# A fused sliding-window attention and gated projection: q and k turned by VectorE, scores in four 32-row parts of TensorE, v loaded in overlapping blocks

## The chip, the cores and the metric

The kernel runs on one core of one Trainium2 chip. The metric is the device time of one launch in microseconds (us), taken over several executions; the profile describes one execution and gives its span from the first to the last instruction. The engines are named as in the profile: PE (TensorE matmuls), PEld (its weight loads), DVE (VectorE), ACT (ScalarE), POOL (GpSimd) and SP (SyncE, which only issues DMAs here).

## The reference

There are 8 batches, 8 heads, 576 positions and a head size of 64. Heads 0 to 3 ("plain") see the last 32 positions; heads 4 to 7 ("dilated") see 32 positions at steps of 4. The attention output of the eight heads, side by side, is x (8 x 576 x 512), which goes into a gated unit: a causal depthwise convolution of 5 taps gives the gate, a 512 x 512 matmul gives the values, and a second one gives the output.

```python
scores = scale * np.matmul(q, k.transpose(0, 1, 3, 2))
mask_plain = (rel >= 0) & (rel < window)                                   # window 32
mask_dil = (rel >= 0) & (rel < window * dilation) & (rel % dilation == 0)  # dilation 4
attn = softmax(np.where(masks, scores, -1e9))
x = matmul(attn, v) as (B, S, H * D)
gate_pre[:, s] = sum over k of conv_w[k] * x[:, s - 4 + k]
out = (sigmoid(gate_pre) * (x @ w_val)) @ w_out
```

## The kernel before

**Order.** Nothing is looped in program order. Each piece of work is a `Task` with an engine (or a choice of two), an assumed duration, a priority, the buffers (`Ten`) that it takes and the tasks that it needs. `Plan.run` is a list scheduler: it picks one task after the other by the earliest start, then by priority, assigns buffers, and the order so found is the order of each engine's queue. Priorities are the batch number plus offsets in `TUNE` by kind of task. Where the plan sees TensorE idle, it puts up to six idle matmuls on a tile `warm` (L803) ahead of a task. All loads and stores go through SP's one queue; a load waits until the third load before it has landed (`depth` 3).

**Attention of one batch.** Work is in blocks of 96 queries against 128 keys (the 96 and 32 before them), six blocks in a sequence; a dilated head is four interleaved sequences of 144 positions. For the plain heads `load_p` (L433) brings q and k as two strips of 2304 bytes per partition; 18 TensorE transposes per tensor (L548) turn them into one PSUM tile, and two copies by ACT or DVE (L465, L467) put them into `qT` and `kT`, two heads to a tile of 128 rows. For the dilated heads `load_d` (L443, L447) brings rows of 1024 bytes, and five transposes (L613) and one copy serve each half. `attend` runs six score matmuls per half sequence, two heads in two 64-row parts of the array (L486), exp on ACT (L493), the mask on DVE or POOL (L500), 12 matmuls with v (L509, the row sums come from an added column of ones), and the reciprocal and scaling on DVE (L518, L519).

**v.** A block needs its 96 rows and the 32 before it. `load_vp` (L458, pieces of 256 bytes) and `load_vd` (L452, pieces of 1024 bytes) bring the 96 rows to partitions 32 to 127; a copy by POOL or ACT (`halo`, L465 or L469) then fills partitions 0 to 31 from partitions 96 to 127 of the block before. The dilated v is cast to bf16 (`vn`).

**Back to rows of x.** Transposes of `xn` (L573, L639) and copies to `xT` follow, one per pair of heads, four per batch.

**Gated unit.** For each half batch of 288 positions and each pair of 128 channels: 20 convolution matmuls (L669), tanh on ACT (L679), 8 value matmuls (L687), and the product on DVE into `yT` (L697). `outputs` takes 128 rows at a time: 4 matmuls with `w_out` (L715), a copy to `osb` (L723, L725), a store of 256 KB (L729); 36 of them.

**PSUM** is three tiles of two banks (`ps2`) and two of one bank (`ps1`).

Of the kernel before, what the change touches and what calls it, by code (L numbers as in the profile page):

```python
# [15 lines left out]


TUNE = {'seed': 193001,
 'jit': 0,
 'lag': 2.021,  # L20
 'plain': 0.646,
 'unit': -0.629,
 'half': -0.321,
 'chunk': 0.345,
 'look': {'PE': 0, 'ACT': 0.233, 'DVE': 0.13, 'POOL': 0.697, 'SP': 0.591},
 'flex': 0.338,
 'switch': 0.02,
 'conv': -1.304,
 'wv': 1.403,
 'wo': 2.062,  # L30
 'bufs': {'ps2': 3,
          'ps1': 2,
          'qk': 8,
          'vp': 3,
# [4 lines left out]
          'et': 5,  # L39
          'xn': 4,  # L40
          'gate': 3,
          'osb': 5,
          'xT': 4,
          'yT': 3},
 'kind': {'G': -0.357,
          'Xd': -1.057,
          'Ad': 0.509,
          'Sp': -4.69,
          'Tqp': -0.992,
          'Ap': -0.173,  # L50
          'Ekd': -1.272,
          'Eqd': 1.89,
          'ST': -1.836,
          'Y': 0.794,
          'Ed': 1.871,
          'Wv': -0.423,
          'Lqd': 0.297,
          'C': -1.069,
          'Lqp': -0.075,
          'Tqd': -1.649,  # L60
          'Lvp': 0.148,
          'Fp': 4.197,
          'U': 2.107,
          'H': 3.76,
          'Ep': -0.793,
          'Md': 1.981,
          'Ct': 3.963,
          'Xp': -0.118,
          'Tkd': 0.572,
          'Fd': -1.123,  # L70
          'Nd': 0.276,
          'Lc': -0.608,
          'Lwo': 2.324,
          'Sd': -0.312,
          'Wo': 1.347,
          'early': 1.617,
          'EO': -0.437,
          'Cd': 1.31,
          'Ekp': -4.677,
          'Tkp': -2.543,  # L80
          'Np': 1.144,
          'Lvd': 0.762,
          'Eqp': -2.532,
          'Lkr': -0.445,
          'Lkp': 0.146,
          'Mp': -2.525,
          'Lqr': 0.066,
          'Lwv': -0.03,
          'Lkd': -0.161,
          'V': -0.623,  # L90
          'O': 0.244},
 'depth': 3,
 'heat': 6,
 'page0': 440,
 'lookq': 3.0}


def hi_bf16(ap: bass.AP) -> bass.AP:
# [15 lines left out]
class Task:  # L114
    def __init__(self, name, eng, fn, deps=(), tens=(), prio=0.0, mode=None, xfer=0.0, n=1, act=0.0, out=None):
        self.name = name
        self.eng = eng
        self.fn = fn
        self.deps = [d for d in deps if d is not None]
        self.tens = [t for t in tens if t is not None]  # L120
# [8 lines left out]
        self.end = None  # L129
        self.users = []  # L130
        self.missing = len(self.deps)
        for d in self.deps:
            d.users.append(self)
        for t in self.tens:
            t.left += 1


class Plan:
# [3 lines left out]
    WIN, HOT, PAGE, FETCH = 3.4134, 0.40, 256, 1.1  # L142
    HEAT = 0.2133

    def __init__(self, counts):
        self.tasks = []
        self.free = {c: [0.0] * n for c, n in counts.items()}
# [7 lines left out]
        self.heats = 0  # L155
        self.act = {}
        self.slow = {}
        self.count = 0
        self.pages = {}
        self.bound = TUNE["page0"]  # L160
        self.rnd = random.Random(TUNE["seed"])

    def add(self, *a, **k):
        t = Task(*a, **k)
        kind = "".join(takewhile(str.isalpha, t.name))
        t.prio += TUNE["kind"].get(kind, 0.0) + self.rnd.uniform(-1.0, 1.0) * TUNE["jit"]
        self.tasks.append(t)
        return t

    def emit(self, t, eng):  # L170
        t.fn(eng)

    def ready(self, t, eng):
        r = 0.0
        for d in t.deps:
            if d.on == SP or d.on == eng:
                e = d.end
            else:
                e = d.end + self.LAT[d.on]
            if e > r:  # L180
                r = e
# [14 lines left out]
    def pe_run(self, s, dur, act, n):  # L196
        t, i0 = s, self.count
        page = (i0 - self.bound) // self.PAGE + 1
        marks = []
        while self.bound + page * self.PAGE <= i0 + n:  # L200
            marks.append(((self.bound + page * self.PAGE - i0) / n, page))
            page += 1
        marks.append((1.0, None))
        done = 0.0
        for frac, p in marks:
            part = max(0.0, frac - done)
            while part > 1e-9:
                w = int(t / self.WIN)
                f = self.speed(w)
                end = (w + 1) * self.WIN  # L210
                need = part * dur * f
                step = min(need, end - t)
                if step < 1e-9:
                    step, end = min(need, self.WIN), end + self.WIN
                g = step / need * part
                self.act[w] = self.act.get(w, 0.0) + act * g
                t += step
                part -= g
            done = max(done, frac)
            if p is not None:  # L220
                t = max(t, self.pages.get(p, 0.0))
                wait = 1.1 + min(max(0.0, self.dma - t), TUNE["lookq"])
                self.pages[p + 1] = t + wait + self.FETCH
        self.count += n
        return t

    def run(self):
        cand = [t for t in self.tasks if t.missing == 0]
# [3 lines left out]
        depth = TUNE["depth"]  # L232
        look, flex, sw = TUNE["look"], TUNE["flex"], TUNE["switch"]
        while n:
            best = None
            for t in cand:
                if t.load and t is not self.loads[0]:
                    continue
                for eng, dur in t.eng.items():
# [9 lines left out]
                    if eng == PE and t.mode != self.mode:  # L249
                        at += sw  # L250
# [10 lines left out]
            after = None  # L261
            if t.load:
                self.loads.pop(0)
                after = self.landed[-depth] if len(self.landed) >= depth else None
                self.landed.append(t)
            gap0 = self.clock[eng]
            for x in t.tens:
                if x.idx is None:
                    f = self.free[x.cls]
                    x.idx = min(range(len(f)), key=lambda i: f[i])  # L270
                    if x is t.tens[0] or x.cls in ("ps1", "ps2"):
# [3 lines left out]
            t.heat = 0  # L275
            if eng == PE:
                if t.out is not None and t.mode is not None:
                    h, at = 0, gap0
                    while h < TUNE["heat"] and at + self.HEAT * self.speed(int(at / self.WIN)) < s - 0.05:
# [4 lines left out]
                        at = self.pe_run(at, self.HEAT, self.HEAT, 2)  # L284
# [5 lines left out]
                    self.heats += h  # L290
                if t.mode != self.mode:
                    s += 0.09
                self.mode = t.mode
                e = self.pe_run(s, dur, t.act, 2 * t.n + 2)
# [19 lines left out]
            self.log.append((s, t.end, eng, t.name))  # L314
            t.after = after
            self.emit(t, eng)
# [3 lines left out]
def kernel(  # L320
# [10 lines left out]
    nc = tc.nc  # L331
    ctx.enter_context(tc.manual_schedule(engines=None))

    B, H, S, D = q.shape
    Dm = moe_w_val.shape[0]
    K = moe_conv_w.shape[0]
    R = 4
    TT = S // R
    RD = R * D
    QB = 96  # L340
    NB = S // QB
    PJ = 9
    PR = S // PJ
    W = 32
    NCH = Dm // 128
    SB = S + 4
    NTOK = B * S
    HW = 288
    DA = D + 1
    scale = 1.0 / float(D) ** 0.5  # L350
    VHEADS = [0, 2, 3, 1, 4, 5, 7, 6]

    N = dict(TUNE["bufs"])
    plan = Plan(N)

# [6 lines left out]
    ps2 = [psum.tile([128, 2, 512], FP32, name=f"pd{i}") for i in range(N["ps2"])]  # L362
    ps1 = [psum.tile([128, 512], FP32, name=f"pu{i}") for i in range(N["ps1"])]
    qk = tiles("qk", [128, 5 * RD], FP32)
    vp = tiles("vp", [128, 4, NB, DA], FP32)
    vd = tiles("vd", [128, NB, RD], FP32)
    vn = tiles("vn", [128, NB, R, DA], BF16)
    qT = tiles("qT", [128, S], BF16)
    kT = tiles("kT", [128, 32 + S], BF16)
    et = tiles("et", [128, 2 * HW + 32], BF16)  # L370
    xn = tiles("xn", [128, NB, 2, D], BF16)
    gate = tiles("gate", [128, 2, HW], BF16)
    osb = tiles("osb", [128, Dm], FP32)
    xT = tiles("xT", [128, NCH, SB], BF16)
    yT = tiles("yT", [128, NCH, 2 * S], BF16)
    warm = consts.tile([128, 512], BF16, name="warm")
    rec = consts.tile([128, 4 * B, 2 * NB], FP32, name="rec")

    ident = consts.tile([128, 128], BF16, name="ident")
    ident2 = consts.tile([128, D], BF16, name="ident2")  # L380
    ident_f = consts.tile([8, 8], FP32, name="ident_f")
    mask = [consts.tile([128, HW], BF16, name=f"mask{i}") for i in range(2)]
    conv_w = consts.tile([128, NCH, K], BF16, name="conv_w")
    conv_diag = consts.tile([128, NCH, K, D], BF16, name="conv_diag")
    w_val = consts.tile([128, NCH, Dm], BF16, name="w_val")
    w_out = consts.tile([128, NCH, Dm], BF16, name="w_out")

    def src_ap(t, offset, ap):
        return bass.AP(tensor=t.tensor, offset=t.offset + offset, ap=ap)

    def early():
        nc.gpsimd.memset(ident, 0.0)
# [459 lines left out]
```

## Time and profile before

| | us |
|---|---|
| three timed executions | 195.63 median, 194.36 to 200.72 |
| span of the profiled execution | 194.1 (the page gives no other time for it) |
| busy: PE, DVE, ACT, POOL | 163.5, 123.6, 106.0, 52.2 |
| granted TensorE clock, mean | 0.935 of full |
| DMA: read, written | 30.42 MB, 9.44 MB |

The rows are shown where the prediction uses them. A busy time is a sum over stages with different limits, so the table alone does not say what a saved microsecond is worth. The DMA share can be over 1 in a short window, since the packets of one DMA engine overlap.

### The profile page before, as it was taken

The numbers are of one execution on the slowest core, as the hardware profiler recorded it, in microseconds if no ns is written. First come the engines' busy times: TensorE is split into PE (matmuls) and PEld (weight loads), VectorE is DVE, ScalarE is ACT, GpSimd is POOL, SyncE is SP. The second block draws the span as 40 slices with busy tenths as digits, with TensorE's granted clock in tenths as the row PEclk, the third lists the DMA queues.
The fourth block names the chain that finished last, engine by engine and source line by source line (L and its number), as shares of the span: only waits on it lengthen the run. The fifth ranks groups of instructions, "written<-read, shape, count | busy, mean of one in ns | idle before, by whom it ended". The sixth has DMA issues, their size and how long they took to land.

```text
span 194.1 us, 6135 instructions
## 1 busy us (share of the span) xinstructions
PE 163.5 (84%) x2625; PEld 115.2 (59%) x2625; DVE 123.6 (64%) x242; ACT 106.0 (55%) x172; POOL 52.2 (27%) x60
## 2 busy tenths in 40 slices
PE   0970798988929988999699989997979998999992
PEld 0540677666716766774467765775556675686650
DVE  7660475778733996784658659873958587755330
ACT  2061378644643467365659558536845828654442
POOL 5002208035160227351522113403225534000000
PEclk9978559997975999999999999999999999999998
DMA  1889798996997899978999998978799812321325
GB/s 56 251 237 168 170 255 233 262 187 175 237 200 216 253 232 175 252 196 222 235 371 330 334 174 298 269 194 167 254 289 311 214 65 76 135 109 57 121 95 216
DMA packets 43778, 40.24 MB, mean 207 GB/s; under 512 B 20195, under 2 KB 34024, under 8 KB 43752
## 3 DMA queue, kind: packets, MB, share of 16 engines
q1 hardware_dynamic: 43752, 39.86, 79.7%
q8 instruction: 20, 0.33, 0.7%
q14 instruction: 6, 0.05, 0.1%
HBM read 30.42 MB, written 9.44 MB: 205 GB/s over the span
## 4 chain that ended last, share of the span: by engine, by line
DMA 58%; PE 33%; ACT 2%; DVE 2%; issue 1%; POOL 1%; SPq 1%; ACTq 0%; POOLq 0%
DMA qk<-in_k_dram 25%; DMA qk<-in_q_dram 13%; PE pu L715 12%; DMA vp<-in_v_dram 8%; PE pd L687 7%; DMA vd<-in_v_dram 6%; PE pd L669 5%; DMA vd<-in_moe_w_out_dram 3%; DMA vd<-in_moe_w_val_dram 3%; PE pd L509 2%; PE pu L613 2%; PE pd L548 2%; PE pd L486 2%; POOL w_out L469 1%; DVE qT L467 1%
## 5 line engine op out<-in xcount | busy, mean ns | idle before, releaser
L493 ACT ACTIVATE et<-pd 128x576 bf16<-128x576 f32 x64 | 37.9, 651 | 15.1 <-PE pd L486 14.0
L715 PE MATMUL pu<-w_out,yT 128*128 128x512 bf16 x144 | 35.3, 379 | 2.3 <-ACT xT L465 1.6
L687 PE MATMUL pd<-xT,w_val 128*128 128x288 bf16 x256 | 36.9, 296 | 0.1
L697 DVE SCALAR_TENSOR_TENSOR yT<-gate,pd 128x576 bf16<-128x576 bf16 x32 | 24.0, 750 | 15.1 <-PE pd L687 15.0
L519 DVE TENSOR_TENSOR xn<-pd,rec 96x768 bf16<-96x768 f32 x32 | 30.5, 954 | 1.1
L723 ACT ACTIVATE osb<-pu 128x512 f32<-128x512 f32 x32 | 19.0, 603 | 20.8 <-PE pu L715 20.4
L687 PEld LDWEIGHTS <-w_val 128*128 128x128 bf16 x256 | 24.7, 101 | 8.5 <-issue 0.8
L500 DVE TENSOR_TENSOR et<-et,mask 128x576 bf16<-128x576 bf16 x51 | 25.9, 536 | 4.9 <-ACT et L493 4.2
L500 POOL TENSOR_TENSOR et<-et,mask 128x576 bf16<-128x576 bf16 x13 | 16.7, 1282 | 37.6 <-ACT et L493 37.5
L669 PE MATMUL pd<-xT,conv_diag 64*64 64x288 bf16 x640 | 23.7, 285 | 1.7 <-ACT et L493 0.9
L679 ACT ACTIVATE gate<-pd 128x576 bf16<-128x576 f32 x32 | 20.5, 654 | 4.5 <-PE pd L669 2.7
L715 PEld LDWEIGHTS <-yT 128*128 128x128 bf16 x144 | 13.1, 97 | 15.4 <-issue 3.2
L548 PE MATMUL pd<-ident,qk 128*64 128x128 bf16 x288 | 11.8, 238 | 11.9 <-DMA qk<-in_k_dram 10.8
L669 PEld LDWEIGHTS <-conv_diag 64*64 64x64 bf16 x640 | 17.6, 106 | 4.5 <-issue 2.5
L486 PE MATMUL pd<-qT,kT 64*128 64x96 bf16 x384 | 16.5, 208 | 4.4 <-DVE xn L519 1.5
L613 PE MATMUL pu<-ident,qk 128*128 128x128 bf16 (+1 forms) x160 | 17.3, 227 | 1.6 <-DMA qk<-in_q_dram 1.0
L548 PEld LDWEIGHTS <-qk 128*64 128x64 bf16 x288 | 9.6, 121 | 14.8 <-DMA qk<-in_k_dram 12.5
L509 PEld LDWEIGHTS <-et 128*128 128x128 bf16 x384 | 16.3, 104 | 3.0 <-issue 0.7
L613 PEld LDWEIGHTS <-qk 128*128 128x128 bf16 (+1 forms) x160 | 11.7, 102 | 9.6 <-DMA qk<-in_k_dram 1.7
L467 DVE COPY kT<-pd 128x576 bf16<-128x576 bf16 x9 | 6.7, 756 | 16.1 <-PE pd L548 11.7
L486 PEld LDWEIGHTS <-kT 64*128 64x128 bf16 x384 | 10.6, 96 | 9.4 <-issue 7.2
L469 POOL CAST vn<-vd 128x1536 bf16<-128x1536 f32 x7 | 10.6, 1516 | 16.8 <-ACT vd L465 16.6
(54 smaller groups left out, 154.0 us busy)
## 6 DMA issues: line engine op xcount, KB each, us to landing
out_dram<-osb SPq DMA_DIRECT2D x36, 256.0 KB, 3.4
qk<-in_q_dram SPq DMA_DIRECT2D x8, 576.0 KB, 5.6
vd<-in_v_dram SPq DMA_DIRECT2D x8, 576.0 KB, 6.6
qk<-in_k_dram SPq DMA_DIRECT2D x8, 576.0 KB, 8.2
vp<-in_v_dram SPq DMA_DIRECT2D x8, 576.0 KB, 8.8
qk<-in_k_dram SPq DMA_DIRECT2D x8, 512.0 KB, 6.1
qk<-in_q_dram SPq DMA_DIRECT2D x8, 512.0 KB, 4.3
vd<-in_moe_w_val_dram SPq DMA_DIRECT2D x4, 256.0 KB, 5.3
```

What stands on the lines that cost most here:

```text
L486: nc.tensor.matmul(out=ps2[ps.idx][:, l, QB * jj:QB * jj + QB], lhsT=kT[kt.idx][rb, c:c + 128], rhs=qT[qt.idx][rb, c:c + QB], start=True, ...
L493: nc.scalar.activation(out=et[e.idx][:, 0:2 * HW].rearrange("p (l n) -> p l n", l=2), in_=ps2[ps.idx][:, :, 0:HW], func=AF.Exp, scale=scale)
L500: (nc.vector if eng == DVE else nc.gpsimd).tensor_tensor(out=ev, in0=ev, in1=m, op=ALU.mult)
L509: nc.tensor.matmul(out=ps2[po.idx][:, hf, (2 * jj + l) * DA:(2 * jj + l + 1) * DA], lhsT=et[es[hf].idx][:, c:c + 128], rhs=val(j, l), star ...
L519: nc.vector.tensor_tensor(out=xn[xt.idx][0:QB].rearrange("p (h j) l d -> p h (j l) d", h=2), in0=a[:, :, :, 0:D], in1=rr[:, :, :, None].to ...
L548: nc.tensor.transpose(out=o[64 * y:64 * y + 64, 128 * j:128 * j + 128], in_=a[:, (y * PJ + j) * D:(y * PJ + j + 1) * D], identity=ident)
L613: nc.tensor.transpose(out=o[:, 128 * c:128 * c + m], in_=a[0:m, c * RD + 128 * cb:c * RD + 128 * cb + 128], identity=ident[0:m, 0:m])
L669: nc.tensor.matmul(out=ps2[pc.idx][64 * ob:64 * ob + 64, n, 0:HW], lhsT=conv_diag[rb, 2 * cp + n, kk, :], rhs=xT[xb.idx][rb, 2 * cp + n, s ...
L679: nc.scalar.activation(out=gate[g.idx], in_=ps2[pc.idx][:, :, 0:HW], func=AF.Tanh, scale=0.5)
L687: nc.tensor.matmul(out=ps2[pv.idx][:, n, 0:HW], lhsT=w_val[:, mc, c * 128:(c + 1) * 128], rhs=xT[xb.idx][:, mc, c0:c0 + HW], start=(mc == ...
L697: nc.vector.scalar_tensor_tensor(out=yT[yb.idx][:, 2 * cp:2 * cp + 2, t0:t0 + HW], in0=gate[g.idx], scalar=1.0, in1=ps2[pv.idx][:, :, 0:HW ...
L715: nc.tensor.matmul(out=ps1[po.idx], lhsT=yT[yb.idx][:, c, c0:c0 + 128], rhs=w_out[:, c, :], start=(c == 0), stop=(c == NCH - 1))
```

## The change

The kernel is rewritten around the same scheduler and the same blocks. What differs:

- **q and k.** Four heads of q (or k) come in one DMA, 4608 bytes per partition (partition p holds rows 18p to 18p+17 of the four heads' 2304 rows). `turn` is one DVE instruction per tensor: a transpose in 32 x 32 blocks of 1152 elements per partition, from every second 16-bit half of the fp32 input, written with a step of 18 elements into `qT` or `kT`. Each 32-row part of these then holds one head's positions for 32 of its 64 dimensions, in two tiles e = 0, 1. The TensorE transposes and the copies out of PSUM go.
- **Scores.** Each head has one 32-row part of the array; the 64 dimensions are summed in two matmuls (e = 0, 1). Four heads run side by side into four PSUM banks, 24 matmuls per plain half sequence and 32 per dilated pair of sequences, so each score task takes two of now four equal PSUM tiles of two banks.
- **v.** Loads bring 128 rows per block, the 32 repeated ones too, straight from memory: 24 x 128 pieces of 256 bytes and 6 x 128 of 1024 bytes per batch. The `halo` copies go.
- **Pairs.** The four `xT` evictions of a batch become two of 1152 elements; 34 of the 36 output tiles go in pairs (17 stores of 512 KB) and the last two alone.
- **Weights** come in `qk` buffers, with priorities that put `w_out` among the loads of batch 1; before, it had a higher number (`'wo'` 2.062 and `'Lwo'` 2.324 against now 1.493).
- **Plan.** `depth` is 4, `lag` 1.429 (was 2.021), all constants in `TUNE` are new, the model of instruction pages is gone, most start-up memsets go from DVE to POOL.

```diff
-    def load_p(src, b, ten, prio, what):
-                in_=src_ap(src, b * H * S * D, [[PJ * D, 128], [2 * S * D, 2], [1, PJ * D]]))
-    def load_d(src, b, ten, prio, what):
-            return nc.sync.dma_start(out=t[:, 0:4, :], in_=src_ap(src, o, [[RD, 128], [128 * RD, 4], [1, RD]]))
...
+    def load_qk(name, src, h0, b, ten, prio):
+        def issue():
+            return nc.sync.dma_start(out=tl.qk[ten.idx],
+                                     in_=src_ap(src(), (b * H + h0) * S * D, [[PJ * D, 128], [1, PJ * D]]))
+        return load(name, [ten], issue, 1.5, prio)
+    def load_vd(b, ten, prio):
+                in_=src_ap(io.v, (b * H + 4) * S * D - W * RD, [[RD, 128], [QB * RD, NB], [1, RD]]))
+    def load_vp(b, ten, prio):
+                    out=o, in_=src_ap(io.v, b * H * S * D - W * D, [[D, 128], [QB * D, 4 * NB], [1, D]]))
...
+    def turn(name, src, dst, off, width, dep, prio):
+        def fn(eng):
+            i = hi_bf16(tl.qk[src.idx]).rearrange("p (j e d) -> p j e d", j=PJ, e=2)
+            t = (tl.qT if dst.cls == "qT" else tl.kT)[dst.idx]
+            o = t[:, :, off:off + S].rearrange("p e (r j) -> p j e r", j=PJ)
+            nc.vector.transpose(out=o, in_=i)
+        return plan.add(name, {DVE: 1.30}, fn, deps=[dep], tens=[src, dst], prio=prio)
...
+                for jj in range(3):
+                    c = QB * (3 * hf + jj)
+                    for e in range(2):
+                        for h in range(4):
+                            rb = slice(32 * h, 32 * h + 32)
+                            nc.tensor.matmul(
+                                out=tl.ps[ps[h // 2].idx][:, h % 2, QB * jj:QB * jj + QB],
+                                lhsT=tl.kT[kt.idx][rb, e, PADF - W + c:PADF - W + c + 128],
+                                rhs=tl.qT[qt.idx][rb, e, c:c + QB], start=(e == 0), stop=(e == 1))
...
-        def halo(eng):
-            copy(eng, vp[tv.idx][0:32, :, 1:NB, 0:D], vp[tv.idx][96:128, :, 0:NB - 1, 0:D])
...
+        def evx(eng):
+            copy(eng, tl.xT[xb.idx][:, 0:2, 4:], tl.ps[px.idx].bitcast(BF16)[:, :, 0:S])
...
+        groups = [(i, 2) for i in range(0, NT - 2, 2)] + [(NT - 2, 1), (NT - 1, 1)]
...
- 'lag': 2.021,
- 'wo': 2.062,
- 'depth': 3,
+ 'lag': 1.429,
+ 'wo': 1.493,
+ 'depth': 4,
```

More of the change, by code (lines that the diff above doesn't have):

```diff
@@ L15 @@
 PE, ACT, DVE, POOL, SP = "PE", "ACT", "DVE", "POOL", "SP"
-TUNE = {'seed': 193001,
- 'jit': 0,
- 'lag': 2.021,
[L21 to L29, printed above, removed]
- 'wo': 2.062,
[L31 to L34, printed above, removed]
+B, H, S, D = 8, 8, 576, 64
+Dm = H * D
+K = 5
+R = 4
+TT = S // R
+RD = R * D
+QB = 96
+NB = S // QB
+W = 32
+NCH = Dm // 128
+SB = S + 4
+NTOK = B * S
+HW = 288
+DA = D + 1
+PJ = 18
+PADF, PADB = 320, 192
+KW = PADF + S + PADB
+TUNE = {'seed': 326090,
+ 'jit': 0.05,
+ 'lag': 1.429,
+ 'plain': 0.38,
+ 'unit': 0.325,
+ 'half': 0.021,
+ 'chunk': 0.476,
+ 'look': {'PE': 0.31, 'ACT': 0, 'DVE': 0.33, 'POOL': 0.18, 'SP': 2.02},
+ 'flex': 0.405,
+ 'wv': 0.848,
+ 'wo': 1.493,
+ 'conv': 0.333,
+ 'depth': 4,
+ 'heat': 6,
+ 'bufs': {'ps': 4,
+          'qk': 7,
+          'vp': 2,
           'vd': 2,
@@ L119, in __init__ @@
         self.deps = [d for d in deps if d is not None]
-        self.tens = [t for t in tens if t is not None]
+        self.tens = list(tens)
         self.prio = prio
@@ L129, in __init__ @@
         self.end = None
+        self.heat = 0
+        self.after = None
         self.users = []
@@ L194, in speed, with pe_run @@
         return s
[L196 to L224, printed above, removed]
+    def pe_run(self, t, dur, act):
+        part = 1.0
+        while part > 1e-9:
+            w = int(t / self.WIN)
+            f = self.speed(w)
+            end = (w + 1) * self.WIN
+            need = part * dur * f
+            step = min(need, end - t)
+            if step < 1e-9:
+                step, end = min(need, self.WIN), end + self.WIN
+            g = step / need * part
+            self.act[w] = self.act.get(w, 0.0) + act * g
+            t += step
+            part -= g
         return t
     def run(self):
+        tune = self.tune
         cand = [t for t in self.tasks if t.missing == 0]
@@ L370 @@
[L370 to L380, printed above, removed]
@@ L800, in emit @@
-    def emit(t, eng):
+    tl, io = Box(), Box()
+    io.q, io.k, io.v, io.w_val, io.conv, io.w_out, io.out = q, k, v, moe_w_val, moe_conv_w, moe_w_out, out
+    tl.ps = [psum.tile([128, 2, 512], FP32, name=f"ps{i}") for i in range(N["ps"])]
+    tl.qk = tiles("qk", [128, PJ * D], FP32)
+    tl.vp = tiles("vp", [128, 4, NB, DA], FP32)
+    tl.vd = tiles("vd", [128, NB, RD], FP32)
+    tl.vn = tiles("vn", [128, NB, R, DA], BF16)
+    tl.qT = tiles("qT", [128, 2, S], BF16)
+    tl.kT = tiles("kT", [128, 2, KW], BF16)
@@ new lines @@
+    tl.ident_f = consts.tile([8, 8], FP32, name="ident_f")
+    tl.mask = [consts.tile([128, HW], BF16, name=f"mask{i}") for i in range(3)]
+    tl.conv_w = consts.tile([128, NCH, K], BF16, name="conv_w")
+    tl.conv_diag = consts.tile([128, NCH, K, D], BF16, name="conv_diag")
+    tl.w_val = consts.tile([128, NCH, Dm], BF16, name="w_val")
+    tl.w_out = consts.tile([128, NCH, Dm], BF16, name="w_out")
+    plan = Plan(TUNE)
+    graph(plan, nc, io, tl)
+    plan.run()
+    for _, _, eng, t in plan.log:
```

875 lines of the change are left out of this document (402 added, 473 removed).

## The prediction, made before the changed kernel was run

> **What bounds the kernel now.** I read the slices of the page first, to see where TensorE and the DMA engines are full, then the chain that ended last.
>
> ```profile
> span 194.1 us, 6135 instructions
> PE 163.5 (84%) x2625; PEld 115.2 (59%) x2625; DVE 123.6 (64%) x242; ACT 106.0 (55%) x172; POOL 52.2 (27%) x60
> PE   0970798988929988999699989997979998999992
> DVE  7660475778733996784658659873958587755330
> DMA  1889798996997899978999998978799812321325
> DMA 58%; PE 33%; ACT 2%; DVE 2%; issue 1%; POOL 1%; SPq 1%; ACTq 0%; POOLq 0%
> ```
>
> The DMA row falls from 9s to 2s about three quarters through; until then TensorE has holes, afterwards none. So there are two stages. The stage windows and the DMA issues in order of time give the border:
>
> ```profile
> 0.00:152.00 152.00, 125.61 (x2074) 89.75 (x2074) 102.82 (x209) 84.13 (x135) 46.43 (x56) 0.92 0.94 232
> 152.00:190.00 38.00, 37.40 (x552) 25.47 (x552) 20.78 (x34) 20.96 (x36) 5.82 (x5) 1.00 0.30 110
> 89.28 5.73 SPq L729 DMA_DIRECT2D out_dram<-osb  x2
> 144.66 0.34 SPq L458 DMA_DIRECT2D vp<-in_v_dram  x1
> 145.83 45.73 SPq L729 DMA_DIRECT2D out_dram<-osb  x19
> 186.16 4.36 PE pu L715 x20
> ```
>
> (Columns of a window: length, busy us of PE, PEld, DVE, ACT and POOL with instructions, granted clock, DMA share, GB/s.) The last load is issued at 144.66 us and has landed by about 152. Up to there the DMA engines are busy to 0.94 and move 232 GB/s; **loads set the pace**. Behind it TensorE works for 37.40 of 38 us: **TensorE sets the tail**, because work has piled up. Stores begin only at 89 us, and 19 of 36 are issued after the last load. A change gains by shortening the load stage, or by leaving less TensorE work behind it.
>
> **TensorE's share of the change.** The instructions that read `qk` (all q/k transposes), those on `qT` and `kT` (scores, and the copies out of PSUM), as sums over the span, and three pieces of the chain:
>
> ```profile
> sum 194.00, PE 28.99 PEld 21.29; mean PE 9.66 PEld 7.10
> sum 194.00, PE 16.53 DVE 10.44 ACT 8.97; mean PE 5.51 DVE 3.48 ACT 2.99
> sum 194.00, PE 16.53 PEld 10.61 DVE 12.32 ACT 7.03; mean PE 5.51 PEld 3.54 DVE 4.11 ACT 2.34
> 154.12 0.23 PE pd L486 x6
> 150.46 0.36 PE pd L486 x12
> 166.44 0.49 PE pd L486 x18
> ```
>
> The transposes go: -29.0 us of PE. Scores grow from 384 to 8 x (2 x 24 + 2 x 32) = 896 matmuls of the same 96 columns, in 32 groups rather than 64. The three pieces give (0.49 - 0.23) / 12 = 21.7 ns per matmul and 0.10 us per group in two array parts. Four parts cost at best half, 10.9 ns, at worst the same 21.7: 3.2 + 896 x 10.9..21.7 ns = 13.0 to 22.6 us against 16.5 now. I take 16 ns, 17.5 us, +1, since the only row for parts is for two. PE becomes 163.5 - 29.0 + 1 = **135.5 us** (131 to 142).
>
> [...]
>
> **DVE's share.** Copies of known size, masks and normalisation:
>
> ```profile
> L467 DVE COPY kT<-pd 128x576 bf16<-128x576 bf16 x9 | 6.7, 756 | 16.1 <-PE pd L548 11.7 <-ACT kT L465 4.4
> L519 DVE TENSOR_TENSOR xn<-pd,rec 96x768 bf16<-96x768 f32 x32 | 30.5, 954 | 1.1
> L500 POOL TENSOR_TENSOR et<-et,mask 128x576 bf16<-128x576 bf16 x13 | 16.7, 1282 | 37.6 <-ACT et L493 37.5
> L469 POOL COPY vp<-vp 32x1280 f32<-32x1280 f32 x7 | 8.8, 1253 | 20.2 <-DMA vp<-in_v_dram 20.2
> L469 POOL COPY vd<-vd 32x1280 f32<-32x1280 f32 x5 | 6.4, 1283 | 26.7 <-DMA vd<-in_v_dram 26.7
> L465 ACT COPY vd<-vd 32x1280 f32<-32x1280 f32 x3 | 3.8, 1256 | 6.7 <-DMA vd<-in_v_dram 6.7
> ```
>
> No row shows a transpose on DVE. Two strided operations do: 576 elements in 756 ns and 768 in 954, so 1.03 ns per element; 1152 elements are 756 + 576 x 1.03 = 1.35 us. If two elements went at once it would be 0.75; if the 36-byte write step halves the rate, 2.5. I take 1.35, the rows' own slope: 32 x 1.35 = +43.2 us. The q/k copies go: -22.8 us (10.44 + 12.32) of DVE and -16.0 of ACT. The larger `xT` and output copies save a few fixed parts, and POOL, freed of 15.2 us of halo copies, can take some ten more masks off DVE; together I put -4. DVE: 123.6 + 43.2 - 22.8 - 4 = **140 us** (120 to 180). ACT loses 16.0 and 3.8 us of halo copies, and is nowhere the bound.
>
> [...]
>
> **The DMA share.** What the size of the pieces does, in one window with a `vp` load (256-byte pieces) under way, and one without:
>
> ```profile
> 56.00:58.00 2.00, 0.00 (x0) 0.00 (x0) 0.00 (x0) 0.00 (x0) 1.94 (x2) 0.54 1.32 154
> 100.00:102.00 2.00, 2.00 (x30) 1.21 (x29) 1.26 (x3) 1.19 (x3) 0.00 (x0) 1.00 1.07 384
> 52.42 0.33 SPq L458 DMA_DIRECT2D vp<-in_v_dram  x1
> SPq L458 <- DMA qk<-in_q_dram: 17.8, 7, 7.0
> vp<-in_v_dram SPq DMA_DIRECT2D x8, 576.0 KB, 8.8
> ```
>
> That `vp` load, issued at 52.42, is one of eight with a median of 8.8 us to landing. DMA engines are full in both windows, at 154 and 384 GB/s. Steps for the load stage of 152 us:
> - `vp` grows by a third, 0.197 MB a batch, 1.57 MB in all, at 154 GB/s: +10.
> - `vd` grows by as much, at the stage's 232 GB/s: +7.
> - q and k are 18.9 MB as before, in pieces of 4608 bytes for 1024 (dilated) and 2304 (plain). Nothing, if size does not matter here; from 232 to 384 GB/s for all of it, 81 to 49 us, -32. The plain half has long pieces already, so I count half of the dilated half's gain (40.7 to 24.6 us): -8.
> - Stores: with `w_out` loaded with batch 1 and a shorter lag, I expect some 26 of 36 before the last load in place of 17: 9 x 0.262 MB at 232 to 384 GB/s, +6 to +10, take +8.
> - Four loads under way rather than three: SP waited 17.8 us on L458 for an earlier load. The stage's 0.94 could go towards 1.07: 0 to -18, take -6.
> Sum: 152 + 10 + 7 - 8 + 8 - 6 = **163 us**, with bounds from 125 to 179.
>
> **What hides the rest.** SP issues six loads a batch rather than eight, but still holds stores in the same queue, so a store that waits for its copy delays the loads behind it. `turn` puts a wait for the load on DVE; behind it in the queue stand masks, `xn`, `yT` and so, through full PSUM tiles, TensorE. Today the same wait stands on TensorE. Start-up is as before: the first scores need both loads and now two 1.35 us turns, in place of two transposes and copies.
>
> **The tail.** After the last load one half batch still needs v matmuls (0.5), reciprocal and scaling (1.2), transposes and copy (1.4), four convolution and value groups of 8 x 0.144 + 20 x 0.037 = 1.9 (7.6), product (0.75), up to 5 output tiles of 0.9 (4.5), a copy and the last store (0.6 + 3): 19.5 us. Those figures are from these rows and the page's issue table (3.4 us to landing):
>
> ```profile
> L687 PE MATMUL pd<-xT,w_val 128*128 128x288 bf16 x256 | 36.9, 296 | 0.1
> L669 PE MATMUL pd<-xT,conv_diag 64*64 64x288 bf16 x640 | 23.7, 285 | 1.7 <-ACT et L493 0.9 <-DVE kT L467 0.5 <-ACT qT L465 0.3
> L697 DVE SCALAR_TENSOR_TENSOR yT<-gate,pd 128x576 bf16<-128x576 bf16 x32 | 24.0, 750 | 15.1 <-PE pd L687 15.0
> L715 PE MATMUL pu<-w_out,yT 128*128 128x512 bf16 x144 | 35.3, 379 | 2.3 <-ACT xT L465 1.6 <-POOL w_out L469 0.6
> ```
>
> No backlog stands behind the load if PE keeps up: 135.5 us in 182 is 74%, where it managed 125.6 in 152 (83%). So the span is 163 + 19 = **182 us**. The median of the three runs is 195.63, 1.5 us over the span of the profile; 182 + 1.5 = 183.5, rounded to **183**.
>
> **Rivals.**
> 1. *Loads run free, an engine binds.* If long pieces and four loads give most of their bounds, loads end near 140 and the busiest engine decides. TensorE is busy 84% of the span now; DVE at 140 / 0.84 is 167 us, 168.5 with the rest. For it: the 384 GB/s window. Against it: that window had output stores in it, too.
> 2. *No change.* Repeated v costs its full 17 us, q and k gain nothing, the depth gains nothing: 152 + 10 + 7 + 8 = 177, plus 19 and 1.5: 197.
> 3. *Slower: DVE becomes the queue that everything stands in.* A late load stops `turn`, and with it masks, scaling and products that need no load. Today's waits for loads on the engine that turns q and k, and DVE's waits:
>
> ```profile
> PEld L548 <- DMA qk<-in_k_dram: 12.5, 5, 6.1
> DVE yT L697 <- PE pd L687: 15.0, 19, 3.4
> DVE kT L467 <- PE pd L548: 11.7, 4, 6.8
> ```
>
> With DVE at 140 busy, 182 leaves it 42 us of idling in all; today it idles 194.1 - 123.6 = 70. If it idles 65 again, since 20 us of start and end stay and loads still come late, the span is 205, time 206. The point is 42 us of idling; above 54 the change loses. A turn of 2.5 us (DVE near 177) gives the same result by another way. Against it: many of today's DVE waits are for TensorE, which gets lighter by 28 us.
>
> **How the numbers follow.** The forecast gets 0.42, rival 1 0.19, rival 2 0.14, rival 3 0.25. The forecast's own range is 174 to 191. The range reaches into the lowest and the highest case: 166 to 206. Faster by over 2% (about what a measurement of this kernel can tell from no change; under 191.7) takes the forecast and rival 1: 0.61; within 2% is rival 2: 0.14; slower is rival 3: 0.25.
>
> **What the new profile would show.** DVE about 140 us with 32 transposes of 1.35; PE about 136; scores at 16 ns per matmul; `vp` loads slower by a third; stores spread from about a third of the span; the last load near 163 and no full TensorE tail behind it. It would be wrong above all if DVE's idle time names loads of q and k in tens of us, if the transposes take other than 1.35 us, or if a third kind of wait shows: score tasks take two of four PSUM tiles, so TensorE could wait for exp. Nor would the sum hold if TensorE, less busy, were granted a lower clock: in the window at 56 us, where it idled, the clock was 0.54.

## The result, and the profile after

The changed kernel takes 278.57 us (median of four, 276.87 to 279.50) against 195.72 before: a ratio of 1.427, 95% interval 1.418 to 1.435. The prediction was 183, with a range of 166 to 206. Times here are medians over all executions, and ratios leave out, for both kernels, those over 1.5% above the fastest of their kernel.

The page of the changed kernel: span and busy times, four of the slice rows, the chain by engine.

```profile
span 277.8 us, 6069 instructions
...
PE 165.2 (59%) x2677; PEld 112.3 (40%) x2691; DVE 234.7 (84%) x169; ACT 99.0 (36%) x142; POOL 67.0 (24%) x84
...
PE   3061817293556729391667499057449197299993
...
DVE  8999999959996999769999949996988959857440
...
PEclk9555675779595977689587869658959869579999
DMA  6997972009859102992039609990245102002215
...
DVE 52%; PE 30%; issue 15%; ACT 1%; DVEq 0%; ACTq 0%
```

Before, the DMA row was full for three quarters of the span, then PE. Now DVE's row is nearly full from the first slice almost to the last, and every other row has holes: the DMA engines stand still in several slices, PE is busy 59%, and its granted clock falls to 5 tenths again and again. DVE holds 52% of the chain, where it had 2%. Three of the groups of instructions (busy us and mean ns of one; then the idle time before them) show on what:

```profile
L376 DVE STREAM_TRANSPOSE qT<-qk 128x1152 bf16<-128x1152 bf16 x16 | 83.5, 5220 | 0.0
L376 DVE STREAM_TRANSPOSE kT<-qk 128x1152 bf16<-128x1152 bf16 x16 | 82.9, 5205 | 0.0
L416 DVE TENSOR_TENSOR xn<-ps,rec 96x768 bf16<-96x768 f32 x32 | 30.5, 954 | 1.2
```

The 32 transposes take 5.2 us each, 166.4 in all, and DVE never idles ahead of one: when it comes to a transpose, the load has landed. The other DVE work is as it was (`xn` again 954 ns). The prediction took 1.35 us per transpose, 3.86 too little: 32 x 3.86 = 124 us of DVE time. What follows from that stands in the waits of SP's queue in the changed kernel (us in all, times, longest):

```profile
SPq L632 <- ACT osb L623: 171.8, 18, 20.9
```

and in the waits of its other engines:

```profile
PE ps L513 <- DVE qT L376: 18.6, 2, 11.1
DVE yT L596 <- PE ps L588: 15.8, 19, 4.1
```

Stores stand in SP's queue until their outputs exist, up to 20.9 us, and the loads behind them stand too (SP issued a load at 86.50 us, nothing more until a store at 107.83, and the next load at 110.27); TensorE waits for `qT`, up to 11.1 us for one.

### The profile page after: what moved, and what is told of

It is laid out like the page before. It is cut to its first block, busy times and chain, and to the rows that moved or that the text cites. A ratio compares the mean times of both kernels' runs of the same rounds, so it can differ in the third digit from the quotient of the medians.

```text
span 277.8 us, 6069 instructions
## 1 busy us (share of the span) xinstructions
PE 165.2 (59%) x2677; PEld 112.3 (40%) x2691; DVE 234.7 (84%) x169; ACT 99.0 (36%) x142; POOL 67.0 (24%) x84
## 2 busy tenths in 40 slices
DMA packets 41605, 43.39 MB, mean 156 GB/s; under 512 B 25701, under 2 KB 31845, under 8 KB 41578
## 4 chain that ended last, share of the span: by engine, by line
DVE 52%; PE 30%; issue 15%; ACT 1%; DVEq 0%; ACTq 0%
DVE kT L376 24%; DVE qT L376 17%; PE ps L588 12%; PE ps L614 7%; PE ps L571 5%; DVE xn L416 4%; PE ps L406 3%; DVE yT L596 3%; PE ps L446 1%; PE ps L513 1%; DVE xT L303 1%; PE ps L470 1%; DVE rec L415 1%; DVE et L395 1%; ACT et L383 0%
## 5 line engine op out<-in xcount | busy, mean ns | idle before, releaser
L395 POOL TENSOR_TENSOR et<-et,mask 128x576 bf16<-128x576 bf16 x43 | 55.3, 1308 | 165.6 <-ACT et L383 95.8
L376 DVE STREAM_TRANSPOSE qT<-qk 128x1152 bf16<-128x1152 bf16 x16 | 83.5, 5220 | 0.0
L376 DVE STREAM_TRANSPOSE kT<-qk 128x1152 bf16<-128x1152 bf16 x16 | 82.9, 5205 | 0.0
L588 PE MATMUL ps<-xT,w_val 128*128 128x288 bf16 x256 | 42.4, 329 | 5.5 <-DVE xT L303 5.5
L571 PE MATMUL ps<-xT,conv_diag 64*64 64x288 bf16 x640 | 30.5, 338 | 18.3 <-DVE xT L303 10.7
L614 PE MATMUL ps<-w_out,yT 128*128 128x512 bf16 x132 | 39.0, 434 | 2.2 <-issue 0.7
L596 DVE SCALAR_TENSOR_TENSOR yT<-gate,ps 128x576 bf16<-128x576 bf16 x32 | 24.1, 761 | 15.9 <-PE ps L588 15.8
L387 ACT ACTIVATE et<-ps 128x576 bf16<-128x576 f32 x32 | 19.0, 653 | 44.2 <-PE ps L446 44.2
L416 DVE TENSOR_TENSOR xn<-ps,rec 96x768 bf16<-96x768 f32 x32 | 30.5, 954 | 1.2
L571 PEld LDWEIGHTS <-conv_diag 64*64 64x64 bf16 x640 | 21.8, 125 | 23.2 <-issue 19.9
L580 ACT ACTIVATE gate<-ps 128x576 bf16<-128x576 f32 x32 | 20.2, 654 | 28.0 <-PE ps L571 27.1
L383 ACT ACTIVATE et<-ps 128x576 bf16<-128x576 f32 x32 | 19.0, 654 | 28.2 <-PE ps L513 28.2
```

What stands on the lines that cost most here:

```text
L376: nc.vector.transpose(out=o, in_=i)
L383: nc.scalar.activation(out=o.rearrange("p (l h t) -> p h l t", l=2, h=2), in_=tl.ps[ps.idx][:, :, 0:HW].rearrange("p h (l t) -> p h l t", ...
L387: nc.scalar.activation(out=o.rearrange("p (l n) -> p l n", l=2), in_=tl.ps[ps.idx][:, :, 0:HW], func=AF.Exp, scale=scale)
L395: (nc.vector if eng == DVE else nc.gpsimd).tensor_tensor(out=ev, in0=ev, in1=m, op=ALU.mult)
L416: nc.vector.tensor_tensor(out=tl.xn[xt.idx][0:QB].rearrange("p (h j) l d -> p h (j l) d", h=2), in0=a[:, :, :, 0:D], in1=rr[:, :, :, None] ...
L571: nc.tensor.matmul(out=tl.ps[pc.idx][64 * ob:64 * ob + 64, n, 0:HW], lhsT=tl.conv_diag[rb, 2 * cp + n, kk, :], rhs=tl.xT[xb.idx][rb, 2 * c ...
```

## The experiments

Three theories stood against each other. A: the transpose's price is all that the sum missed. B: something else in the rewrite costs as well (score tasks that hold half of PSUM, stores in the loads' queue, the order of the plan). C: the price is not the transpose's own but comes from its surroundings. Each kernel is compared with runs of the kernel before on the same chip.

**What a transpose costs alone.** A kernel with nothing but forms of transposes and copies, which computes nothing of the reference:

```diff
+    for _ in range(N):
+        nc.vector.transpose(out=out18, in_=in4)        # as in the changed kernel
+    for _ in range(N):
+        nc.vector.transpose(out=out18, in_=dn4)        # dense input
+    for _ in range(N):
+        nc.vector.transpose(out=flat, in_=src_h)       # dense output
+    for _ in range(N):
+        nc.vector.transpose(out=flat, in_=dense)       # both dense
...
```

> This kernel computes nothing of the reference: it loads one strip of q and runs forms of the DVE transpose and of copies six times each, one after the other, with nothing beside them, and stores zeros. Theory 1, the write step: a transpose that writes 2-byte elements 36 bytes apart pays some 4 cycles per element; with the same step a plain copy pays it too (about 5 us), and a transpose to a dense output takes 1.35 us. Theory 2, the price is per 32 x 32 block (36 blocks of 0.145 us): every transpose of 1152 elements takes 5.2 us whatever its steps, 576 elements 2.6, 128 elements 0.6, and plain copies stay at or under 1.4. Theory 3, the read step of 4 bytes: dense inputs bring it to 1.35. Theory 4, contention inside the kernel: the form of the changed kernel takes 1.35 us here.

Rows from the groups of instructions of this kernel (busy us and mean ns of one; idle time before):

```profile
L45 DVE STREAM_TRANSPOSE strided<-src 128x1152 bf16<-128x1152 bf16 x6 | 30.4, 5072 | 0.0
L47 DVE STREAM_TRANSPOSE strided<-dense 128x1152 bf16<-128x1152 bf16 x6 | 30.3, 5048 | 0.0
L49 DVE STREAM_TRANSPOSE flat<-src 128x1152 bf16<-128x1152 bf16 x6 | 9.2, 1536 | 0.0
L51 DVE STREAM_TRANSPOSE flat<-dense 128x1152 bf16<-128x1152 bf16 x6 | 8.1, 1353 | 0.0
L53 DVE STREAM_TRANSPOSE flat<-dense 128x576 bf16<-128x576 bf16 x6 | 4.4, 726 | 0.0
L57 DVE STREAM_TRANSPOSE wide<-dense 128x1152 bf16<-128x1152 bf16 x6 | 8.4, 1404 | 0.0
L61 DVE COPY strided<-src 128x1152 bf16<-128x1152 bf16 x6 | 15.8, 2642 | 0.0
L63 DVE COPY strided<-dense 128x1152 bf16<-128x1152 bf16 x6 | 45.5, 7582 | 0.2
L65 DVE COPY strided<-flat 128x1152 bf16<-128x1152 bf16 x6 | 15.8, 2629 | 0.2
```

With the step of 36 bytes between writes (`strided`) a transpose takes 5.07 us with no other engine computing (ACT and POOL idled for 114 us ahead of their copies), so the surroundings are out (C, and the expectation's theory 4). The input's step is worth nothing there (5.05 with a dense input), a price per block is out too (36 blocks to a dense output take 1.35). The write step is the cause. (`flat<-src` shows 1.54 here and 1.34 in the next kernel: here each stood between two strided transposes, and the recorded lengths overlap: a strided one of 5.05 us starts at 39.68 us, and the one after it at 44.38.) But theory 1 missed in one thing: a plain copy with the same steps takes 2.64, half of the transpose's time, so the step costs a transpose more than a copy. The copies of L63 took 7.58: they ran beside copies with the same write step on POOL and ACT, and the same form after those had ended (L65) took 2.63 again. So copies can be held up by what runs beside them; the run with copies in place shows it again.

**The step, swept.** Two, three, six, nine and eighteen elements between writes; 1152 elements in 9, 6, 3, 2 and 1 instructions:

```diff
+    def turn(j):
+        i = src_h.rearrange("p (g j e d) -> p g j e d", j=j, e=2, d=32)
+        o = dst.rearrange("p e (g r j) -> p g j e r", r=32, j=j)
+        for g in range(18 // j):
+            nc.vector.transpose(out=o[:, g], in_=i[:, g])
```

> Computes nothing of the reference: forms of the DVE transpose one after the other, then copies, then a mask product on POOL alone, beside transposes and beside DVE copies; zeros are stored. The first such kernel showed 1.54 us for a transpose of 1152 elements to a dense output, 1.40 with a write step of 4 bytes and 5.07 with 36 bytes. Theory 1 (the price grows with the distance of the writes): steps of 2, 3, 6, 9 and 18 elements give a rising row, near 1.5 at 2 and 5.1 at 18, the steps between them somewhere on the way. Theory 2 (one threshold, each write that lands apart from the last pays the same): 2 is quick and all others cost about 5 us in total. For the copies: a copy that writes densely and reads with the step costs 1.4 or less on DVE and 1.1 on ACT, if only writes pay. For POOL: beside DVE copies its product takes about 2.5 us in place of 1.3, beside transposes 1.3, if it is the DVE copies that held it up in the run with copies for transposes.

Rows from its groups, with the same columns, in the order of the steps; `dst` is written with the step, `flat` is dense:

```profile
L48 DVE STREAM_TRANSPOSE flat<-src 128x1152 bf16<-128x1152 bf16 x6 | 8.1, 1342 | 4.6 <-DMA src<-in_q_dram 4.6
L42 DVE STREAM_TRANSPOSE dst<-src 128x128 bf16<-128x128 bf16 x54 | 11.0, 280 | 0.0
L42 DVE STREAM_TRANSPOSE dst<-src 128x192 bf16<-128x192 bf16 x36 | 11.5, 458 | 0.0
L42 DVE STREAM_TRANSPOSE dst<-src 128x384 bf16<-128x384 bf16 x18 | 23.0, 1532 | 0.0
L42 DVE STREAM_TRANSPOSE dst<-src 128x576 bf16<-128x576 bf16 x12 | 30.4, 2861 | 0.0
L42 DVE STREAM_TRANSPOSE dst<-src 128x1152 bf16<-128x1152 bf16 x6 | 30.6, 5099 | 0.2
L64 DVE COPY dst<-flat 128x1152 bf16<-128x1152 bf16 x6 | 6.8, 1132 | 0.2
L68 ACT COPY cact<-cact 128x1152 bf16<-128x1152 bf16 x6 | 12.7, 2122 | 0.2
L66 ACT COPY cact<-dst 128x1152 bf16<-128x1152 bf16 x6 | 30.7, 5112 | 155.2 <-DVE dst L64 155.0
```

An instruction has about 0.1 us of its own (1.353 us for 1152 dense elements, 0.726 for 576). The rest per element: 1.1 ns dense, 1.1 at a step of 2 elements by the long instruction of the first kernel (`wide`, 1404 ns for 1152), then at most (458 - 100) / 192 = 1.9 at 3, 3.7 at 6, 4.8 at 9 and 4.3 at 18. For the short instructions these are upper values, because their lengths overlap: the 36 at a step of 3 kept DVE busy for 11.5 us in all, 0.32 each, which by the same working is 1.1, so that a step of 3 costs little or nothing. The price is there at 6 and full at 9: theory 1, with a ceiling. Reading with a step of 64 bytes and writing densely is cheap on DVE (1.13 us) and dearer than expected on ACT (2.12, not 1.1); ACT pays 5.11 when it writes with the step.

**The transposes as copies, in place.** One word of the changed kernel:

```diff
-            nc.vector.transpose(out=o, in_=i)
+            nc.vector.tensor_copy(o, i)
```

> The changed kernel with one word changed: the 32 DVE transposes become plain copies with the same patterns, so q and k are not turned and the scores are of mixed dimensions; everything else is as before. Theory A: the transpose's price is all that failed in the sum; if the copies take about 1.35 us, DVE is near 140 us busy and the span comes to 175 to 191. Rival B: a second cause stands behind it (PSUM held by score tasks, or stores that hold loads back in SP's queue); the span stays above 200 though DVE falls to 140. If the copies take 5 us as well, the price is the write step's and the span stays near 278.

212.14 us, ratio 1.092 (1.076 to 1.108). The copies took 2.97 us on average, not 1.35, so the run could not test the sum as it was meant to. It showed something else, in the groups of the masks on POOL and of the copies on DVE:

```profile
L395 POOL TENSOR_TENSOR et<-et,mask 128x576 bf16<-128x576 bf16 x43 | 106.8, 2507 | 47.5 <-ACT et L383 35.4
L376 DVE COPY qT<-qk 128x1152 bf16<-128x1152 bf16 x16 | 47.5, 2969 | 0.0
```

and in the chain by engine on the page of this run:

```profile
PE 42%; POOL 31%; DVE 11%; issue 7%; ACT 5%; POOLq 2%; ACTq 0%
```

A mask on POOL took 2.5 us in place of 1.3 and POOL came to 31% of the chain. In the kernel of the sweep the same product took 1.27 us on POOL alone, 1.27 beside transposes and 3.45 beside DVE copies (its groups, in that order):

```profile
L72 POOL TENSOR_TENSOR ma<-ma,mask 128x576 bf16<-128x576 bf16 x6 | 7.6, 1270 | 0.5
L76 POOL TENSOR_TENSOR ma<-ma,mask 128x576 bf16<-128x576 bf16 x12 | 15.3, 1274 | 0.9
L82 POOL TENSOR_TENSOR ma<-ma,mask 128x576 bf16<-128x576 bf16 x6 | 20.7, 3448 | 0.5
```

So the substitute brought a cost of its own that the transposes do not have.

**Dense writes, in place.** The cleaner test: the same transposes, the same plan, only the output's order changed.

```diff
-            o = t[:, :, off:off + S].rearrange("p e (r j) -> p j e r", j=PJ)
+            o = t[:, :, off:off + S].rearrange("p e (j r) -> p j e r", j=PJ)
```

> The changed kernel with the 32 transposes writing 32 elements side by side (positions of a head stand in another order in qT and kT, so that the window masks fall on other positions: the scores are of other pairs); all else is as it was, the plan too. Theory A (the write step is the whole of what the prediction missed): turns of 1.54 us, DVE 235 - 32 x 3.67 = 117 us busy, span 175 to 190, near the 183 predicted. Rival B (something else in the changed kernel costs as well, such as stores in SP's queue or PSUM): above 195.

168.54 us, ratio 0.858 (0.850 to 0.866): 110 us less than the changed kernel, from the place of 32 x 1152 writes. Its page, span, busy times and two slice rows:

```profile
span 164.7 us, 6081 instructions
...
PE 142.4 (86%) x2691; PEld 98.7 (60%) x2691; DVE 122.9 (75%) x169; ACT 98.2 (60%) x142; POOL 67.6 (41%) x84
...
PE   6165977998999999889999979799888999999990
...
DMA  5999999999999999999899999999990303006035
```

The group of the transposes of q in that run:

```profile
L376 DVE STREAM_TRANSPOSE qT<-qk 128x1152 bf16<-128x1152 bf16 x16 | 21.8, 1360 | 2.0 <-DMA qk<-in_q_dram 1.5
```

The last load among SP's issues in order of time (start, length):

```profile
113.37 0.38 SPq L364 DMA_DIRECT2D vp<-in_v_dram  x1
```

And two stage windows (length, busy us of PE, PEld, DVE, ACT and POOL, clock, DMA share, GB/s):

```profile
0.00:125.00 125.00, 107.35 (x2175) 75.58 (x2175) 105.33 (x140) 78.28 (x115) 66.08 (x83) 0.99 1.03 317
125.00:164.00 39.00, 35.01 (x526) 23.13 (x516) 17.54 (x30) 19.94 (x28) 1.57 (x2) 0.95 0.25 97
```

The transposes take 1.36 us. The two stages are back: the DMA row full, then PE. B falls in the sum: whatever else in the rewrite may cost, its other parts gain more. The run even came in under the predicted span; its terms are taken up below.

**The plan told the truth.** The scheduler had assumed 1.30 us.

```diff
-        return plan.add(name, {DVE: 1.30}, fn, deps=[dep], tens=[src, dst], prio=prio)
+        return plan.add(name, {DVE: 5.20}, fn, deps=[dep], tens=[src, dst], prio=prio)
```

> The changed kernel with the plan told 5.2 us per transpose in place of 1.30; the work is the same, its order is new. Theory A: DVE is the bound and its work cannot shrink: about 235 us busy, plus some 5 us ahead and 15 to 20 behind, so 255 at the very best, a gain of 0 to 23 us. Rival: the wrong order is the larger part of the loss; then the span falls below 250.

254.54 us (two runs), ratio 1.307. DVE was 225.1 us busy of 254.5. The new order, which also gave POOL 59 masks in place of 43, was worth 24 us of the 83 lost, at the edge of theory A. The granted clock was 0.912 in this run in place of 0.773, and the kernel still took far longer than the one before, so the low clock does not explain the loss.

**v alone.** The kernel before, with the overlapping loads and without the halo copies:

```diff
-            return nc.sync.dma_start(out=vd[ten.idx][32:128],
-                              in_=src_ap(v, (b * H + 4) * S * D, [[RD, QB], [QB * RD, NB], [1, RD]]))
+            return nc.sync.dma_start(out=vd[ten.idx],
+                              in_=src_ap(v, (b * H + 4) * S * D - W * RD, [[RD, 128], [QB * RD, NB], [1, RD]]))
...
-        t_h = plan.add(f"H{b}", {POOL: 1.35, ACT: 1.25}, halo, deps=lv, tens=[tv], prio=prio)
```

> The kernel before with one part of the change alone: v is loaded in overlapping blocks over 128 partitions, a third mask zeroes the first block's halo, and the halo copies go. By the prediction's term: 3.1 MB more to read, +17 us of load stage, so about 205 to 212 us in place of 195.7. Rival: the DMA engines have room, and POOL and ACT lose 20 us of copies that stood between a load and its use: 190 to 198.

189.97 us, ratio 0.975 (0.966 to 0.985): a gain where the prediction had +17 us. The window of the first 150 us in the kernel before:

```profile
0.00:150.00 150.00, 123.61 (x2043) 88.49 (x2045) 100.99 (x206) 82.42 (x133) 45.77 (x55) 0.92 0.93 232
```

and in the one with overlapping v:

```profile
0.00:150.00 150.00, 129.55 (x2166) 92.12 (x2167) 101.81 (x207) 88.18 (x146) 34.22 (x48) 0.95 0.94 266
```

The DMA share is the same and the rate is 266 GB/s in place of 232: more bytes at no more time, and 6 us more of TensorE work done by then. A kernel of loads alone was to price each kind:

> Computes nothing of the reference: each kind of load four times, one at a time, each waited for by a small DVE copy; zeros are stored. The prediction's price: loads cost by bytes and by the size of their pieces, so v in 128 rows takes a third longer than in 96 (plain: 3072 pieces of 256 bytes against 2304; dilated 768 of 1024 bytes against 576), and q or k in rows of 4608 bytes up to 40 percent less than in rows of 1024. Rival: 128 partitions take as long as partitions 32 to 127, and pieces of 1024 bytes or more cost alike by the byte.

The DMA issues of this kernel (KB of each, median us from issue to landing; 576 KB is 96 rows of v and 768 is 128; `big` is plain v in pieces of 256 bytes), and DVE's waits for two single loads of dilated v, the last into 96 partitions and the first into 128:

```profile
big<-in_v_dram SPq DMA_DIRECT2D x4, 576.0 KB, 5.2
big<-in_v_dram SPq DMA_DIRECT2D x4, 768.0 KB, 5.7
vd<-in_v_dram SPq DMA_DIRECT2D x4, 576.0 KB, 5.7
vd<-in_v_dram SPq DMA_DIRECT2D x4, 768.0 KB, 4.9
qk<-in_q_dram SPq DMA_DIRECT2D x8, 576.0 KB, 3.8
qk<-in_q_dram SPq DMA_DIRECT2D x4, 512.0 KB, 3.8
...
67.68 0.20 DVE L45 COPY seen<-vd 128x64 f32<-128x64 f32 x1 [4.79 <-DMA vd<-in_v_dram]
72.61 0.20 DVE L48 COPY seen<-vd 128x64 f32<-128x64 f32 x1 [4.74 <-DMA vd<-in_v_dram]
```

The loads did not run quite alone: the stores of zeros were under way beside all those of plain v, and beside the first three of dilated v into 96 partitions, so that the median of 5.7 there says little. Plain v had stores beside it in both forms, and a third more rows cost it 0.5 us, not the 1.3 that 0.197 MB takes at 154 GB/s. Dilated v without stores kept DVE waiting 4.79 us for 96 rows and 4.74 to 5.24 for 128: little or nothing. For q, pieces of 1024 bytes take 3.8 us for 512 KB, and the two longer forms 3.8 for 576: about an eighth by the byte, not the 40% that was the bound. How much of the gain in place came from the loads and how much from the halo copies, which went in the same run, stays open.

**The depth.** Four loads under way, in the kernel before, and three, in the changed one with dense writes; one number each in `TUNE`.

> The kernel before with four loads under way rather than three, nothing else (the plan's order follows from it). By the prediction's term the load stage loses about 6 us, at most 18: 178 to 193. Rival: the depth is worth nothing, 194 to 199.

192.77 us, ratio 0.986 (0.979 to 0.992).

> The changed kernel with dense turns (scores of other pairs, as before) and three loads under way rather than four. If the depth is what lets its loads run at more than before's 232 GB/s: 174 to 186 in place of 168.5. If the longer pieces do it: 166 to 172.

172.77 us (two runs) against 168.54, ratios to the kernel before 0.882 and 0.858. The depth is worth some 3 to 5 us in both. With three loads the same 43.39 MB as with four, in a span of 170.5 us, are 254 GB/s (an estimate from the run's span and the bytes on the page of the run with four), against 263 over the span with four and 207 in the kernel before: most of the higher rate is not the depth's. No run tells apart what the long pieces of q and k and the loads of v in 128 partitions gave to it.

**Both gains put together.** The loads of v and the depth in the kernel before:

> The kernel before with overlapping v and four loads under way, both of which gained when alone (ratios 0.975 and 0.986). If they relieve different things the ratio is about 0.961, 188 to 190 us; if both relieve the same stretch (loads kept from starting, then TensorE full to the end) it is 0.97 to 0.98.

185.28 us, ratio 0.957 (0.942 to 0.973), near the product of the two, 0.961: they seem to add up, though the interval still touches 0.97. And the changed kernel with a dense transpose and a copy that puts the positions in order, first by ACT or DVE, then by POOL too:

```diff
...
+            nc.vector.transpose(out=tl.tT[mid.idx], in_=hi_bf16(tl.qk[src.idx]))
+        t1 = plan.add(name, {DVE: 1.36}, fn, deps=[dep], tens=[src, mid], prio=prio)
+        def order(eng):
...
+            copy(eng, t[:, :, off:off + S].rearrange("p e (r j) -> p e r j", j=PJ),
+                 tl.tT[mid.idx].rearrange("p (j e r) -> p e r j", j=PJ, e=2))
+        return plan.add("P" + name, {ACT: 2.15, DVE: 1.15}, order, deps=[t1], tens=[mid, dst], prio=prio)
```

> The changed kernel with the transposes writing densely into a new tile, and 32 copies, by ACT (2.1 us) or DVE (1.1), which read with the step of 32 elements and write densely into qT and kT in the right order: the whole reference is computed. Against the run with dense turns alone (168.5): DVE at 123 and ACT at 98 us busy take some 50 us more between them. Theory (DVE and ACT have room, DMA and PE bind at 165): 172 to 186. Rival (DVE near 75 percent is full already, and one more step stands between load and scores): 187 to 200.

188.79 us, ratio 0.962 (0.952 to 0.973): the rival's number. DVE and ACT, 139.4 and 141.6 us busy, are both near 75%.

> The changed kernel with dense turns and ordering copies as before (188.8, DVE and ACT both at 140 us busy), with POOL allowed for the copies at an assumed 2.4 us; POOL was busy for 26 percent only. If POOL's copies cost about that and ACT falls below 120: 178 to 186. If POOL's strided reads cost more, or its copies and DVE's hold each other up as the mask products and DVE copies did: 188 to 200.

181.05 us (four runs, 179.08 to 183.56, against a median of 195.94, 192.05 to 200.77, before on the same chip; no interval was formed). POOL took 14 of the 32 copies and ACT fell to 125.0 us busy. Its page:

```profile
PE 148.1 (83%) x2707; PEld 100.8 (57%) x2707; DVE 138.1 (78%) x181; ACT 125.0 (70%) x157; POOL 90.0 (51%) x89
```

and the group of the nine copies of k on POOL:

```profile
L306 POOL COPY kT<-tT 128x1152 bf16<-128x1152 bf16 x9 | 20.0, 2228 | 7.9 <-DVE tT L376 7.9
```

That is the fastest kernel here that computes the reference: the parts of the change are worth 7 to 8%, and the form of one instruction's output turned them into a loss of 43%.

## Why the prediction was wrong

**The step that failed** is the price of `turn` in "DVE's share": 1.35 us by the slope of two rows, with 2.5 as the upper end "if the 36-byte write step halves the rate". It is 5.21. The rows that I took the slope from do not write like that: by the kernel's code both write their elements side by side. The copy into `kT` (756 ns) reads PSUM with a step of 128 elements, and the trace before has the dilated heads' copy of the same size, which reads without a step:

```profile
L467 DVE COPY kT<-pu 128x576 bf16<-128x576 bf16 x12 | 5.5, 455 | 3.6 <-PE pu L613 3.4
```

So that copy was slow because of what it reads (756 ns against 455), and neither row has a price for a step in the writes. That 1.35 us is also what a dense transpose takes (1353 ns) is luck. The guess for the step was a factor of two; it is nearly four. The forecast's upper end for DVE, 180 us, was broken by that alone (234.7), and with it the range: at 84% of the span, the ratio that the busiest engine had, 234.7 us are 279. The text had the way ("A turn of 2.5 us (DVE near 177) gives the same result by another way") but stopped pricing where the row ended.

Point by point, with the run with dense writes where the price of the turn would hide the rest:

- *TensorE 135.5 us*: 142.4 there. Scores were 11.7 and 7.8 us in their two lines, 19.5 for a predicted 17.5 (13.0 to 22.6): inside the range, but in part by luck. It is 19.5 / 896 = 21.8 ns per matmul, or 18.2 without the predicted 3.2 us for the groups, in place of 16, although 256 of the 896 have 48 columns and not the 96 that the sum gave to all. The other 5 us are not taken apart.
- *Granted clock*: named as a danger, and it came: 0.773 over the changed kernel, 0.975 with dense writes. Value matmuls took 42.4 us in the changed kernel in place of 36.9, and 35.2 with dense writes.
- *DVE 140 us with a turn of 1.35*: 122.9. The plan gave POOL 43 masks, where I counted on some 23.
- *Load stage 163 us*: the last load was issued at 113 us, and by 125 the stage was over, at 317 GB/s: the lower bound of the sum, where the forecast had assumed the old rate for most of the bytes. The term for `vp` and `vd`, +17, had the wrong size, as the runs with v alone show. The price of 154 GB/s came from one window in which the load of v was the last of three; the kernel of loads does not show it. The depth's term (-6) had the right sign, against 3 to 5 measured; what the term of long pieces (-8) was worth is not shown.
- *Stores, 26 of 36 ahead of the last load*: 20.
- *Tail 19 us, no backlog*: 40 us, with TensorE 35.01 of 39 us busy. Loads that ended by 125 us, and not at 163, left more behind them. The two errors, 38 us too long and 21 too short, had opposite signs, so that 182 looks nearer to the 164.7 than its terms are.
- *DVE idles for loads of q and k* (rival 3's sign): it did not. Rival 3 gave the right side for another reason. Rival 1 (168) has the number of the kernel whose turn costs what I had assumed, but not its reason: there TensorE, at 86%, is the busiest engine, and DVE, from which the 168 was worked out, stands at 75%.
- *Score tasks hold PSUM*: no wait of any weight shows it in the dense run.

## What to carry to other kernels

Price an instruction by how it writes as well as by how many elements it moves: if no row of the trace writes with that step, the upper end is not a factor of two (here it was 5.07 us against 1.35 written densely), and forty lines of a kernel that runs nothing else settle it. When a transpose must scatter, let it write densely and put the order into a later read, on whichever engines have room (here 181.05 us for the whole kernel against 278.57). A third more bytes cost little here where the same DMA then filled partitions that it had left out (plain v landed in 5.7 us for 5.2); whether the copies between a load and its use were what the loads waited for, no run here tells.

## What was not expected of the hardware

- A DVE transpose of 1152 2-byte elements took 5.10 us at a write step of 36 bytes, 4.3 ns per element, against 1.35 us and 1.1 ns dense; a DVE copy took 2.6 us for the same elements, an ACT copy 5.1; with the step in the read instead, 64 bytes and dense writes, DVE took 1.13 us and ACT 2.12.
- DVE copies held POOL's mask products up: 1.27 us alone or beside transposes, 3.45 beside copies, which themselves went from 2.63 to 3.33 us; a DVE copy and a POOL copy side by side, both written with the step, took 7.6 each, with ACT copies beside them for part of the time. By what means is not shown; a transpose beside the products showed no such hold (1.27 us).
- Loads of v into 128 partitions landed nearly as soon as into partitions 32 to 127: dilated v kept its reader waiting 4.74 to 5.24 us against 4.79, and plain v took 5.7 us to land against 5.2.
